# Layer-2 results of a mixture-of-experts kernel: through a DRAM scratch in 4 writes and 3 reads per expert, with the clearing of three PSUM banks at another place

## The chip, the cores and the metric

One core of a Trainium2 chip runs the whole program. The metric is the device time of one execution in microseconds (us); lower is better. Of each kernel some executions are timed, and one more is profiled.

## What is computed

The program is a linear attention followed by a mixture of 16 experts (4 groups of 4). Every token goes to exactly one expert, picked by two argmax steps. Cut to what matters here:

```
kv  = einsum('bhsd,bhse->bhde', k, v);  out = einsum('bhsd,bhde->bhse', q, kv)
x   = (out / rms(out) * g_norm), as 4608 tokens of 512 features
g   = argmax(x @ w_group);  e = argmax(x @ w_expert[g])          # one expert per token
out[token] = gate * (max(x[token] @ w1[g, e], 0) @ w2[g, e])     # 512 -> 1024 -> 512
```

All inputs and the output are float32. Each expert has 4 MB of weights.

## The kernel before

**Order of the work.** The attention and the routing come first, in an order that a planner writes out. Then the experts are taken by rank, that is by the number of their tokens: rank r is given room for CAPS[r] tokens, from 384 (rank 0) down to 256 (rank 15), and what is beyond goes to a loop at the end that does nothing on this input. Most of rank 0 is computed while the attention ends; what is left of it (128 tokens) and ranks 1 to 15 are the second part, which begins at line 1311. There the order of instructions on each engine is that in which the code is written.

**One rank** (loop at line 1376) has a layer 1 and a layer 2, each of 96 matmuls. A float32 product is made of three products of rounded values: ScalarE makes the rounded part (`whi`, `xh`, `hh`) and VectorE the rest (`wlo`, `xl`, `hl`). Layer 1 goes over 8 chunks f of the hidden features into PSUM tiles `ps`. Layer 2 (`layer2_by_feature`, line 1292) goes over 4 blocks d of the output features: 24 matmuls into one of three PSUM banks `psy`, in turn, then VectorE turns the block by 32 x 32 squares into the SBUF tile `yq` (line 1303). There is one `yq`, so the first such transpose of a rank waits until the results of the rank before have been moved out of it. In the order of VectorE the transposes stand between the splits of the next rank's weights and rows.

**The rows of x.** Three ranks are under way at any time. In layer 1 of rank r GpSimd gathers the rows of rank r+2 (`gather`), multiplies them by their factors (`scale`), and SyncE writes them to a DRAM scratch `xd` (`put_x`, 3 DMAs). At the start of layer 1 of rank r SyncE reads the rows of rank r+1 back as `xq` (`get_x`, 4 DMAs, in pieces of 512 bytes), so laid out that VectorE's transposes by squares (`turn_x`) make a whole transpose of it.

**The results.** `yq` holds the results of a rank by squares. `move_y` (line 1270) brings them to rows, `yo3`, by 16 DMAs from SBUF to SBUF in pieces of 512 bytes, and GpSimd scatters the rows of `yo3` to the output (`scatter_rows`), in layer 1 of the next rank, at f = 5 to 7. There are two `yo3`.

**The weights** come as four DMAs of 1 MB per rank (`wr`; `load_half`, line 207). Their 12 buffers are shared by the loaded and the split halves, so some loads wait until older ones are free: in layer 1 of rank r the two halves of w2 of rank r+1 are loaded (`load_next`), at the end of its layer 2 the two halves of w1 of rank r+2 (`load_a`).

**SyncE's queue** issues all of these DMAs but the gathers and scatters, in the written order. In a rank it is: 4 reads of `xq`, 16 moves of `yq`, 3 writes of `xd`, 2 loads of w2, then 2 loads of w1. Eight semaphores take turns for its DMAs, so a DMA waits at its issue until the one eight before it has landed.

**The banks.** The transposes take whole squares of 32 tokens, so they read up to 31 columns that no matmul wrote. Lines 1358 and 1359 clear columns 256 to 383 of the three banks once, after VectorE has prepared the rows of rank 1 (`turn_x`, `split_x`) and ahead of the last product of rank 0 (line 1364), 32 matmuls (line 299) that write the same banks.

Of the kernel before, what the change touches and what calls it, by code (L numbers as in the profile page):

```python
# [9 lines left out]
F32 = mybir.dt.float32  # L10
# [11 lines left out]
CAPS = [384, 364, 354, 330, 326, 312, 302, 300, 292, 290, 284, 274, 268, 264, 260, 256]  # L22
# [33 lines left out]
def tile_linattn_moe(ctx: ExitStack, tc: tile.TileContext, qm, qt, k, v, router, w1, w2, out):  # L56
    nc = tc.nc
    P = 128
    B, H, S, D = BATCH, HEADS, SEQ, HEAD_DIM
    NTOK, DM = out.shape  # L60
# [179 lines left out]
    def split_piece(w, p):  # L240
        for x, hi, lo in quarter(w, p):
            nc.scalar.copy(out=hi, in_=x)  # L242
            nc.vector.tensor_tensor(out=lo, in0=x, in1=hi.bitcast(F32), op=ALU.subtract)  # L243

    def blocks(cap):
        return [(j, min(P, cap - j * P)) for j in range((cap + P - 1) // P)]
# [5 lines left out]
    def scatter_rows(yo, rows, idx):  # L252
        sc = nc.gpsimd.indirect_dma_start(  # L253
            out=out, out_offset=bass.IndirectOffsetOnAxis(ap=idx[0:rows, :], axis=0), in_=yo[0:rows, :],
            in_offset=None, bounds_check=NTOK - 1, oob_is_err=False)
        tc.declare_no_dep(sc.ins, group=osc, reason="each token has a row of its own")
        tc.add_to_no_dep_group(osc, sc.ins)
# [3 lines left out]
    def by_quarter(x):  # L261
        return x.rearrange("p (a c i) -> p a c i", a=4, c=KC)

    def by_chunk(x):
        return x.rearrange("p (c a i) -> p a c i", a=4, i=32)

    def factors(x):

        return x[:, DM:RW].rearrange("p (c h) -> p h c", h=2).unsqueeze(2).unsqueeze(4).to_broadcast([P, 2, 2, KC, 32])

    def scale_rows(eng, xg, out_=None):

        x = by_quarter(xg[:, 0:DM])
        out_ = x if out_ is None else by_chunk(out_)
        for h in range(2):
            hs = slice(2 * h, 2 * h + 2)
            eng.tensor_tensor(out=out_[:, hs], in0=x[:, hs], in1=factors(xg)[:, h], op=ALU.mult)  # L277

    def split_h(hh, hl, ps):
        nc.scalar.activation(out=hh, in_=ps, func=AF.Relu)  # L280
        nc.vector.scalar_tensor_tensor(out=hl, in0=ps, scalar=0.0, in1=hh.bitcast(F32), op0=ALU.max, op1=ALU.subtract)  # L281

    def layer1(ps, w1, f, xh, xl):
        cs = slice((f % 4) * P, (f % 4 + 1) * P)
        _, wh, wl = w1[f // 4]
        three(ps, KC, lambda c: wh[:, c, cs], lambda c: wl[:, c, cs], lambda c: xh[:, c, :], lambda c: xl[:, c, :])
# [852 lines left out]
    with ExitStack() as ph:  # L1139
# [79 lines left out]
        psys = [ps_q.tile([P, 512], F32, name=f"psy{i}", tag=f"psy{i}") for i in range(3)]  # L1219
# [5 lines left out]

        def moves(cap):

            part = [slice(32 * i, 32 * i + 32) for i in range(4)]  # L1230
            return [(a, s_, part[a], part[s_], len(range(s_, (cap + 31) // 32, 4)))
                    for k in range(4) for s_ in range(4) for a in [(s_ + k) % 4]]

        def gather(r):
            xg = mp.tile([P, 3, RW], F32, name="xg")
            for j, _ in blocks(CAPS[r]):
                st["gather"] = gather_rows(xg[:, j], P, gidx[:, r, j:j + 1])
            xh = mp.tile([P, KC, 384], F32R, name="xh")
            xl = mp.tile([P, KC, 384], F32R, name="xl")
            return xg, xh, xl  # L1240

        def scale(r, g):
            for j, _ in blocks(CAPS[r]):
                scale_rows(nc.gpsimd, g[0][:, j])

        def put_x(r, g):
            for j, rows in blocks(CAPS[r] + -CAPS[r] % 32):
                nc.sync.dma_start(xd[r % 2][j * P:j * P + rows, :], g[0][0:rows, j, 0:DM])

        def get_x(r):  # L1250
            n = (CAPS[r] + 31) // 32
            xq = mp.tile([P, 12, P], F32, name="xq", bufs=1)
            for a in range(4):
                nc.sync.dma_start(xq[32 * a:32 * a + 32, 0:n, :],
                                  xd[r % 2][0:32 * n, a * P:(a + 1) * P].rearrange("(b i) f -> i b f", i=32))
            return xq, mp.tile([P, KC, 384], F32, name="xt", bufs=1)

        def turn_x(r, xq, xt, c):
# [4 lines left out]
        def split_x(r, g, xt, c):  # L1263

            x, xh, xl = (y[:, c, 0:CAPS[r]] for y in (xt, g[1], g[2]))
            nc.scalar.activation(out=xh, in_=x, func=AF.Copy, scale=g2[:, 0:1])  # L1266
            nc.vector.scalar_tensor_tensor(out=xl, in0=x, scalar=g2[:, 0:1], in1=xh.bitcast(F32), op0=ALU.mult,  # L1267
                                           op1=ALU.subtract)

        def move_y(r, yq):  # L1270
            yo = mp.tile([P, 3 * DM], F32, name="yo3", tag="yo3").rearrange("p (j f) -> p j f", j=3)
            pq = yq.rearrange("p (j s) f -> p j s f", s=4)
            for a, s_, pa, ps_, n in moves(CAPS[r]):
                nc.sync.dma_start(yo[ps_, 0:n, a * P:(a + 1) * P], pq[pa, 0:n, s_, :])  # L1274
            return [(yo[:, j], rows, gidx[:, r, j:j + 1]) for j, rows in blocks(CAPS[r])]

        def layer2_by_token(r, w2, hh, hl, side):
# [42 lines left out]
        scale_rows(nc.vector, xr, xs)  # L1320
        for j, _ in blocks(CAPS[1]):
            scale_rows(nc.vector, cur[0][:, j])
        put_x(1, cur)
        xq, xt = get_x(1)
        for i in range(2, 4):
            load_next(i)
# [28 lines left out]
        for c in range(KC):  # L1355
            turn_x(1, xq, xt, c)
            split_x(1, cur, xt, c)
        for x in psys:
            nc.vector.memset(x[:, DM // 2:384], 0.0)
        yo = mp.tile([P, DM], F32, name="yo", bufs=2)  # L1360
        for hf in range(2):
            ps = next_psy()
# [11 lines left out]
        todo, results = None, []  # L1374
        tables = overflow_tables()
        for r in range(1, NE):
            cap = CAPS[r]
            _, xh, xl = cur
            hh = mp.tile([P, FC, 384], F32R, name="hh", bufs=1)
            hl = mp.tile([P, FC, 384], F32R, name="hl", tag="hl", bufs=1)  # L1380
            if nxt:
                xq, xt = get_x(r + 1)
            if todo:
                results = move_y(*todo)
            for f in range(FC):
                if f in w1_at:
                    split_piece(w1c, w1_at[f])
                if f in w2_at:
                    split_piece(w2c, w2_at[f])
                ps = ps_h.tile([P, 512], F32, name="ps")  # L1390
                layer1(ps[:, 0:cap], w1c, f, xh[:, :, 0:cap], xl[:, :, 0:cap])
                split_h(hh[:, f, 0:cap], hl[:, f, 0:cap], ps[:, 0:cap])
                if r > 1:
                    next(tables, None)
                    next(tables, None)
                if f == 0:
                    nxt2 = gather(r + 2) if r + 2 < NE else None
                if nxt2 and f == 1:
                    scale(r + 2, nxt2)
                    put_x(r + 2, nxt2)  # L1400
                if nxt and f in (3, 5):
                    load_next((f + 1) // 2)
                if f >= 5 and results:
                    scatter_rows(*results.pop(0))
                if f == FC - 1 and r + 1 == NE:
                    nc.gpsimd.drain()
            nw1a, nw2a, load_a = weight_loads(eidx[0:1, r + 2:r + 3]) if nxt2 else (None, None, None)
            w1_at, w2_at = {}, {0: 0, 2: 1, 4: 2, 6: 3}

            def side(n, total, after):  # L1410
                if nxt is None:
                    return
                if not after:
                    split_piece(nw1, n)
                    if n < 2:
                        turn_x(r + 1, xq, xt, 2 * n)
                        turn_x(r + 1, xq, xt, 2 * n + 1)
                else:
                    for c in ([0], [1, 2], [3], [])[n]:
                        split_x(r + 1, nxt, xt, c)  # L1420
                    if n >= 2 and nxt2:
                        load_a(n - 2)

            if r + 1 == NE:
                layer2_by_token(r, w2c, hh, hl, side)
            else:
                todo = layer2_by_feature(r, w2c, hh, hl, side)
            cur, w1c, w2c = nxt, nw1, nw2
            nxt, nw1, nw2, load_next = nxt2, nw1a, nw2a, load_a
# [3 lines left out]
    with ExitStack() as ph:  # L1433
# [4 lines left out]
        with tc.For_i(0, nv, 1) as it:  # L1438
# [52 lines left out]
            yo = op.tile([P, DM], F32, name="yoo")  # L1491
# [57 lines left out]
```

## Time and profile before

| | us |
|---|---|
| median of 3 timed runs | 629.09 |
| lowest and highest of them | 622.66 and 629.69 |
| the profiled execution's own time | 625.29 |
| its span, first to last instruction | 623.6 |
| TensorE busy with matmuls | 562.0 (90%) |
| VectorE, ScalarE, GpSimd busy | 375.3, 267.2, 210.3 |
| mean granted TensorE clock | 0.954 |
| DMA, 156.70 MB | 251 GB/s |

The profile is of one execution. In its tables PE is TensorE, PEld its weight loads, DVE VectorE, ACT ScalarE, POOL GpSimd, SP SyncE; SPq is SyncE's sequencer with its DMA issues. A row of the waits gives an engine and a line, whom it waited for, the total in us, how often, and the longest. In a timeline a row has its start and its length in us, then engine, line, operation and tiles; square brackets hold the idle time before it and who ended it. A table of windows gives for each stretch the busy time of each engine with its instructions, then the granted clock (1.00 is full), the busy share of the 16 DMA engines, and what they moved.

### The profile page before, as it was taken

Reading aid. Unit: us, or ns where it says so; the run is one execution under the profiler, and the core shown is the slowest. Engines: PE = TensorE matmul, PEld = TensorE weight load, DVE = VectorE, ACT = ScalarE, POOL = GpSimd, SP = SyncE. Lnnn points to the kernel's source line nnn. Section 1 sums busy time; section 2 is a strip of 40 time slices with the busy share of each in tenths; the row PEclk is TensorE's granted clock in tenths of the full one; section 3 lists DMA queues with packets and bytes.
Section 4 is the critical chain, followed back from the end, with each engine's and each line's share of the span. In section 5 each row is a group of like instructions: output and inputs, shape, how many; then the busy total and the mean of one; then the engine's idle time right before and its main releaser. Section 6 shows DMA issues by size and latency. Waiting matters only on the chain.

```text
span 623.6 us, 13421 instructions
## 1 busy us (share of the span) xinstructions
PE 562.0 (90%) x5181; PEld 521.1 (84%) x5199; DVE 375.3 (60%) x786; ACT 267.2 (43%) x534; POOL 210.3 (34%) x281
## 2 busy tenths in 40 slices
PE   8888869999499999999999998979898979898895
PEld 4666757587189999999999997979898979798895
DVE  4235895862527686777677674657566565658470
ACT  0355645612225344544455453534353435345360
POOL 4032323245226235243144343334334243411103
PEclk9898999999889999999999999979998979798999
DMA  8999995648867769596959595969687777859541
GB/s 297 388 410 359 379 376 190 227 164 263 284 200 253 214 190 313 165 344 172 309 148 353 160 336 183 306 195 286 207 281 261 216 277 204 312 145 354 128 136 68
DMA packets 76788, 156.70 MB, mean 251 GB/s; under 512 B 10194, under 2 KB 49442, under 8 KB 65714
## 3 DMA queue, kind: packets, MB, share of 16 engines
q1 hardware_dynamic: 68752, 133.66, 66.3%
q0 software_dynamic: 7824, 22.11, 10.0%
q8 instruction: 42, 0.69, 0.4%
q10 hardware_dynamic: 146, 0.04, 0.1%
q14 instruction: 24, 0.20, 0.1%
HBM read 117.74 MB, written 29.31 MB: 236 GB/s over the span
## 4 chain that ended last, share of the span: by engine, by line
DMA 37%; PE 36%; SPq 14%; DVE 7%; issue 5%; ACT 1%; POOL 0%; POOLq 0%; DVEq 0%
DMA xq<-xd 20%; SPq L1274 12%; DMA wr<-in_w_dram 7%; PE warm L368 4%; DMA yo<-yq 3%; PE ps L311 3%; PE ps L307 3%; PE ps L306 3%; PE psy L311 3%; PE psy L307 3%; PE ops L521 3%; PE psy L306 3%; PE l L295 2%; DVE wlo L243 2%; PE kps L474 2%
## 5 line engine op out<-in xcount | busy, mean ns | idle before, releaser
L243 DVE TENSOR_TENSOR wlo<-wr,whi 128x1024 fp32r<-128x1024 f32 (+1 forms) x180 | 156.2, 895 | 36.6 <-ACT whi L242 34.4
L306 PE MATMUL psy<-hh,whi 128*128 128x364 f32 (+13 forms) x448 | 141.3, 315 | 22.4 <-DVE yq L1303 22.4
L307 PE MATMUL ps<-xl,whi 128*128 128x364 f32 (+14 forms) x480 | 144.2, 300 | 1.3 <-DVE xl L1267 1.3
L306 PE MATMUL ps<-xh,whi 128*128 128x364 f32 (+14 forms) x480 | 144.1, 300 | 0.4 <-DVE hl L281 0.3
L311 PE MATMUL ps<-xh,wlo 128*128 128x364 f32 (+14 forms) x480 | 144.2, 300 | 0.0
L307 PE MATMUL psy<-hl,whi 128*128 128x364 f32 (+13 forms) x448 | 140.3, 313 | 0.0
L311 PE MATMUL psy<-hh,wlo 128*128 128x364 f32 (+13 forms) x448 | 140.2, 313 | 0.0
L242 ACT CAST whi<-wr 128x1024 fp32r<-128x1024 f32 (+1 forms) x180 | 129.8, 757 | 19.5 <-DMA wr<-in_w_dram 19.5
L253 POOL DMA_INDIRECT out_dram<-yo,gall x45 | 47.9, 1064 | 204.4 <-DMA xd<-xg 99.8
L306 PEld LDWEIGHTS psy<-hh,whi 128*128 128x128 f32 x448 | 89.8, 201 | 24.2 <-DVE yq L1303 24.2
L280 ACT ACTIVATE hh<-ps 128x364 fp32r<-128x364 f32 (+14 forms) x120 | 49.8, 419 | 99.4 <-PE ps L311 97.2
L307 PEld LDWEIGHTS ps<-xl,whi 128*128 128x128 f32 x480 | 90.5, 189 | 1.8 <-DVE xl L1267 1.8
L306 PEld LDWEIGHTS ps<-xh,whi 128*128 128x128 f32 x480 | 90.9, 189 | 0.8 <-DVE hl L281 0.8
L277 POOL TENSOR_TENSOR xg<-xg 128x256 f32<-128x256 f32 x82 | 59.9, 755 | 93.2 <-DMA xg<-scr,gall 93.1
L311 PEld LDWEIGHTS ps<-xh,wlo 128*128 128x128 f32 x480 | 90.6, 189 | 0.0
L307 PEld LDWEIGHTS psy<-hl,whi 128*128 128x128 f32 x448 | 89.9, 201 | 0.0
L311 PEld LDWEIGHTS psy<-hh,wlo 128*128 128x128 f32 x448 | 89.8, 200 | 0.0
L1266 ACT ACTIVATE xh<-xt,rw 128x364 fp32r<-128x364 f32 (+14 forms) x60 | 32.6, 543 | 118.3 <-DVE xt L1260 105.3
L281 DVE SCALAR_TENSOR_TENSOR hl<-ps,hh 128x364 fp32r<-128x364 f32 (+14 forms) x120 | 54.8, 463 | 39.5 <-ACT hh L280 36.4
L1303 DVE STREAM_TRANSPOSE yq<-psy 128x320 f32<-128x320 f32 (+3 forms) x56 | 28.4, 508 | 80.1 <-DMA yo<-yq 62.9
L249 POOL DMA_INDIRECT xg<-scr,gall x44 | 57.3, 1302 | 13.3 <-issue 13.1
L368 PE MATMUL warm<-wide_b,ones_b 128*128 128x512 bf16 x124 | 37.0, 428 | 4.1 <-POOL wide_b L102 2.2
(255 smaller groups left out, 588.3 us busy)
## 6 DMA issues: line engine op xcount, KB each, us to landing
wr<-in_w_dram SPq DMA_DIRECT2D x64, 1024.0 KB
scr<-xo SPq DMA_DIRECT2D x36, 256.0 KB
m_q<-in_qm_dram SPq DMA_DIRECT2D x8, 1024.0 KB
xd<-xg SPq DMA_DIRECT2D x32, 256.0 KB
m_k<-in_k_dram SPq DMA_DIRECT2D x7, 1024.0 KB
m_v<-in_v_dram SPq DMA_DIRECT2D x7, 1024.0 KB
yo<-yq SPq DMA_DIRECT2D x116, 48.0 KB
yo<-yq SPq DMA_DIRECT2D x108, 32.0 KB
```

The source lines that it names most:

```text
L242: nc.scalar.copy(out=hi, in_=x)
L243: nc.vector.tensor_tensor(out=lo, in0=x, in1=hi.bitcast(F32), op=ALU.subtract)
L249: return nc.gpsimd.indirect_dma_start(out=xg[0:rows, 0:RW], out_offset=None, in_=src, in_offset=bass.IndirectOffsetOnAxis(ap=idx[0:rows, : ...
L253: sc = nc.gpsimd.indirect_dma_start(out=out, out_offset=bass.IndirectOffsetOnAxis(ap=idx[0:rows, :], axis=0), in_=yo[0:rows, :], in_offset ...
L277: eng.tensor_tensor(out=out_[:, hs], in0=x[:, hs], in1=factors(xg)[:, h], op=ALU.mult)
L280: nc.scalar.activation(out=hh, in_=ps, func=AF.Relu)
L281: nc.vector.scalar_tensor_tensor(out=hl, in0=ps, scalar=0.0, in1=hh.bitcast(F32), op0=ALU.max, op1=ALU.subtract)
L306: nc.tensor.matmul(ps, lhsT=stat_h(c), rhs=mov_h(c), start=(c == 0), stop=False)
L307: nc.tensor.matmul(ps, lhsT=stat_h(c), rhs=mov_l(c), start=False, stop=False)
L311: nc.tensor.matmul(ps, lhsT=stat_l(d), rhs=mov_h(d), start=False, stop=(d == n - 1))
L368: nc.tensor.matmul(st["warm"], lhsT=ones_b, rhs=wide_b, start=True, stop=True)
L1274: nc.sync.dma_start(yo[ps_, 0:n, a * P:(a + 1) * P], pq[pa, 0:n, s_, :])
```

## The change

Two things are edited. First, `move_y` and its table of 16 moves go. In their place `put_y` writes `yq` to one of two new DRAM scratches `yd` by 4 DMAs, at the place where `move_y` stood, and `get_y` reads it back into `yo3` as whole rows of 2 KB by 3 DMAs (128, 128 and the rest of the rows), at f = 2 of layer 1. `put_x` of rank r+2 moves from f = 1 to f = 4, behind the first load of w2. Second, the clearing of the banks moves from behind `split_x` of rank 1 to a place ahead of `put_x` of rank 1.

```diff
+    yd = [tc.dram_tile([3 * P, DM], F32, name=f"yd{i}") for i in range(2)]
...
-        def moves(cap):
-
-            part = [slice(32 * i, 32 * i + 32) for i in range(4)]
-            return [(a, s_, part[a], part[s_], len(range(s_, (cap + 31) // 32, 4)))
-                    for k in range(4) for s_ in range(4) for a in [(s_ + k) % 4]]
+        def quarter_rows(x, cap, a):
+            n = (cap + 31) // 32
+            return x[0:32 * n, a * P:(a + 1) * P].rearrange("(b i) f -> i b f", i=32)
...
-        def move_y(r, yq):
+        def put_y(r, yq):
+            for a in range(4):
+                nc.sync.dma_start(quarter_rows(yd[r % 2], CAPS[r], a), yq[32 * a:32 * a + 32, 0:(CAPS[r] + 31) // 32, :])
+
+        def get_y(r, yq):
             yo = mp.tile([P, 3 * DM], F32, name="yo3", tag="yo3").rearrange("p (j f) -> p j f", j=3)
-            pq = yq.rearrange("p (j s) f -> p j s f", s=4)
-            for a, s_, pa, ps_, n in moves(CAPS[r]):
-                nc.sync.dma_start(yo[ps_, 0:n, a * P:(a + 1) * P], pq[pa, 0:n, s_, :])
+            for j, rows in blocks(CAPS[r]):
+                nc.sync.dma_start(yo[0:rows, j], yd[r % 2][j * P:j * P + rows, :])
             return [(yo[:, j], rows, gidx[:, r, j:j + 1]) for j, rows in blocks(CAPS[r])]
...
             scale_rows(nc.vector, cur[0][:, j])
+        for x in psys:
+            nc.vector.memset(x[:, DM // 2:384], 0.0)
         put_x(1, cur)
...
             split_x(1, cur, xt, c)
-        for x in psys:
-            nc.vector.memset(x[:, DM // 2:384], 0.0)
         yo = mp.tile([P, DM], F32, name="yo", bufs=2)
...
             if todo:
-                results = move_y(*todo)
+                put_y(*todo)
...
                     scale(r + 2, nxt2)
-                    put_x(r + 2, nxt2)
+                if todo and f == 2:
+                    results = get_y(*todo)
                 if nxt and f in (3, 5):
                     load_next((f + 1) // 2)
+                if nxt2 and f == 4:
+                    put_x(r + 2, nxt2)
```

`get_x` uses `quarter_rows` too and does what it did.

The first place is SyncE's queue at the start of layer 1 of rank 2, with what each DMA waits for beside the order of the queue (DMAHW0 to DMAHW7 are the eight semaphores in turn; `xq<-xd` reads rows, `yo<-yq` moves results). Before:

```order
L1254 DMA xq<-xd_59 32x11x128 [waits DMAHW2_49,DMAHW1_49,DMAHW7_49,DMAHW0_49,DVE_49]
L1254 DMA xq<-xd_59 32x11x128 x3
L1274 DMA yo_2910<-yq 32x3x128 [waits DMAHW3_49,DVE_49]
L1274 DMA yo_2910<-yq 32x3x128 [waits DMAHW4_49]
L1274 DMA yo_2910<-yq 32x3x128 [waits DMAHW5_49]
L1274 DMA yo_2910<-yq 32x3x128 [waits DMAHW6_49]
L1274 DMA yo_2910<-yq 32x3x128 [waits DMAHW7_49]
L1274 DMA yo_2910<-yq 32x3x128 [waits DMAHW0_49]
L1274 DMA yo_2910<-yq 32x3x128 [waits DMAHW1_49]
L1274 DMA yo_2910<-yq 32x3x128 [waits DMAHW2_49]
```

Each move takes the next semaphore of the eight; the other eight moves follow in the same way, and each of those waits for one of the first eight. The same place in the changed kernel:

```order
L1253 DMA xq<-xd_59 32x11x128 [waits DMAHW3_49,DMAHW2_49,DMAHW7_49,DMAHW1_49,DVE_49]
L1253 DMA xq<-xd_59 32x11x128 [waits DMAHW0_49]
L1253 DMA xq<-xd_59 32x11x128 x2
L1270 DMA yd_61<-yq 32x12x128 [waits DVE_49]
L1270 DMA yd_61<-yq 32x12x128 [waits DMAHW4_49]
L1270 DMA yd_61<-yq 32x12x128 [waits DMAHW5_49]
L1270 DMA yd_61<-yq 32x12x128 [waits DMAHW6_49]
L1275 DMA yo_2994<-yd_61 128x512 [waits DMAHW6_49,DMAHW5_49,DMAHW7_49,DMAHW4_49,DMAHW3_49]
L1275 DMA yo_2994<-yd_61 128x512 [waits DMAHW0_49]
L1275 DMA yo_2994<-yd_61 108x512 [waits DMAHW1_49]
```

Four writes follow the reads of `xq`, and the first read of results waits for all four of them; whatever comes later in the queue waits behind it.

The second place is the same queue further on, from the results of rank 1 to the load of the index of the expert of rank 4 (`TENSOR_LOAD`; `xd<-xg` writes rows, `wr` is a half of w2). Before:

```order
L1274 DMA yo_2910<-yq 32x3x128 x16
L1248 DMA xd_58<-xg 128x512 x2
L1248 DMA xd_58<-xg 96x512
L209 ISA
L209 DMA wr_3026<-in_w_dram 128x2048
L209 ISA
L209 DMA wr_3072<-in_w_dram 128x2048
L204 TENSOR_LOAD eidx
```

And in the changed kernel:

```order
L1270 DMA yd_61<-yq 32x12x128 x4
L1275 DMA yo_2994<-yd_61 128x512 x2
L1275 DMA yo_2994<-yd_61 108x512
L210 ISA
L210 DMA wr_3016<-in_w_dram 128x2048
L1247 DMA xd_58<-xg 128x512 x2
L1247 DMA xd_58<-xg 96x512
L210 ISA
L210 DMA wr_3065<-in_w_dram 128x2048
L205 TENSOR_LOAD eidx
```

23 DMAs stand here and at the reads of `xq` before (4, 16, 3) and 14 now (4, 4, 3, 3), and the first half of w2 stands ahead of the writes of rows.

The third place is VectorE's queue between the scaling of the rows of rank 1 and its layer 1 (`hT` is what the last product of rank 0 reads, `psy` are the banks). Before:

```order
L1346 COPY hT<-ps 128x4x128 x2
L1260 STREAM_TRANSPOSE xt<-xq 128x384
L1267 SCALAR_TENSOR_TENSOR xl<-xt,rw,xh 128x364
L1260 STREAM_TRANSPOSE xt<-xq 128x384
L1267 SCALAR_TENSOR_TENSOR xl<-xt,rw,xh 128x364
L1260 STREAM_TRANSPOSE xt<-xq 128x384
L1267 SCALAR_TENSOR_TENSOR xl<-xt,rw,xh 128x364
L1260 STREAM_TRANSPOSE xt<-xq 128x384
L1267 SCALAR_TENSOR_TENSOR xl<-xt,rw,xh 128x364
L1359 MEMSET psy_2443 128x128
L1359 MEMSET psy_2444 128x128
L1359 MEMSET psy_2442 128x128
```

In the changed kernel:

```order
L278 TENSOR_TENSOR xg<-xg 128x256 x6
L1325 MEMSET psy_2444 128x128
L1325 MEMSET psy_2445 128x128
L1325 MEMSET psy_2446 128x128
L244 TENSOR_TENSOR wlo<-wr_2463,whi 128x4x256 x2
L1349 COPY hT<-ps 128x4x128 x2
L1258 STREAM_TRANSPOSE xt<-xq 128x384
```

The three clearings have moved ahead of the two splits, the two copies of `hT` and all eight steps on the rows. On TensorE, ScalarE and GpSimd the order is as before.

More of the change, by code (lines that the diff above doesn't have):

```diff
@@ L1253, in get_x @@
             for a in range(4):
-                nc.sync.dma_start(xq[32 * a:32 * a + 32, 0:n, :],
-                                  xd[r % 2][0:32 * n, a * P:(a + 1) * P].rearrange("(b i) f -> i b f", i=32))
+                nc.sync.dma_start(xq[32 * a:32 * a + 32, 0:n, :], quarter_rows(xd[r % 2], CAPS[r], a))
             return xq, mp.tile([P, KC, 384], F32, name="xt", bufs=1)
```

## The prediction

> **What bounds the kernel now.** I read the page first, then a table of windows cut at the first matmul of each rank's layer 1, then the waits, then one rank in the timeline and the chain.
>
> The page says that TensorE is nearly full, and that its clock is not always full in the second half:
>
> ```profile
> PE 562.0 (90%) x5181; PEld 521.1 (84%) x5199; DVE 375.3 (60%) x786; ACT 267.2 (43%) x534; POOL 210.3 (34%) x281
> ...
> PEclk9898999999889999999999999979998979798999
> ```
>
> The table shows where. One row per rank, here ranks 3 to 15:
>
> ```profile
> core 0: us, PE busy (x) PEld busy (x) DVE busy (x) ACT busy (x) POOL busy (x), PEclk, DMA share, GB/s
> 246.66:275.27 28.61, 28.61 (x195) 28.61 (x193) 21.01 (x48) 13.52 (x24) 9.53 (x10) 1.00 0.78 246
> 275.27:304.06 28.79, 28.79 (x194) 28.79 (x193) 19.71 (x40) 13.55 (x24) 8.21 (x8) 1.00 0.83 232
> 304.06:331.46 27.40, 27.40 (x195) 27.40 (x194) 19.80 (x32) 13.43 (x24) 10.70 (x12) 1.00 0.76 218
> 331.46:357.91 26.45, 26.45 (x195) 26.45 (x194) 16.40 (x29) 11.81 (x22) 8.12 (x11) 1.00 0.77 241
> 357.91:386.88 28.97, 26.51 (x194) 26.26 (x193) 17.50 (x32) 12.30 (x24) 10.93 (x12) 1.00 0.79 251
> 386.88:420.13 33.25, 28.78 (x195) 28.30 (x194) 20.42 (x37) 14.63 (x28) 13.17 (x15) 0.90 0.80 254
> 420.13:448.34 28.21, 26.37 (x195) 26.13 (x194) 16.56 (x29) 11.64 (x23) 11.06 (x11) 1.00 0.76 237
> 448.34:478.53 30.19, 27.26 (x195) 26.79 (x194) 19.52 (x35) 14.26 (x27) 12.34 (x14) 0.94 0.80 262
> 478.53:509.34 30.81, 26.62 (x195) 26.41 (x193) 18.42 (x34) 12.96 (x24) 12.08 (x13) 0.89 0.76 241
> 509.34:538.90 29.56, 26.59 (x194) 26.37 (x193) 18.36 (x34) 12.90 (x24) 13.05 (x13) 0.89 0.77 248
> 538.90:568.00 29.10, 25.75 (x194) 25.12 (x193) 16.79 (x31) 12.38 (x24) 6.96 (x8) 0.93 0.75 245
> 568.00:594.65 26.65, 24.83 (x194) 24.62 (x193) 17.12 (x34) 12.87 (x25) 2.97 (x3) 0.94 0.73 232
> 594.65:623.60 28.95, 21.93 (x194) 21.73 (x192) 10.21 (x21) 8.65 (x21) 4.89 (x5) 0.96 0.27 85
> ```
>
> Up to rank 6 TensorE is busy in every microsecond, and a rank takes time in proportion to its tokens: 111.25 us for the 330 + 326 + 312 + 302 = 1270 tokens of ranks 3 to 6, or 0.0876 us a token. From rank 7 on the tokens go on falling, from 300 to 260, but a rank keeps taking some 27 to 33 us: something of constant length sets the pace. The waits name it:
>
> ```profile
> DVE yq L1303 <- DMA yo<-yq: 62.9, 10, 7.6
> ...
> PE psy L306 <- DVE yq L1303: 22.4, 8, 4.2
> ...
> PE psy L299 <- DVE psy L1359: 10.3, 1, 10.3
> ```
>
> TensorE waits for VectorE's transposes into `yq`, and they wait for the moves out of `yq`. Rank 9 in the timeline of SyncE's queue:
>
> ```profile
> 412.17 1.49 SPq L1248 DMA_DIRECT2D xd<-xg  x3
> 413.93 2.71 SPq L209 DMA_DIRECT2D wr<-in_w_dram  x4
> 416.82 5.33 SPq L1254 DMA_DIRECT2D xq<-xd  x4
> 422.32 20.38 SPq L1274 DMA_DIRECT2D yo<-yq  x16
> 442.81 1.48 SPq L1248 DMA_DIRECT2D xd<-xg  x3
> ```
>
> From the chain of work that ended last, the last move of the rank before and the reads of `xq` (from issue to landing):
>
> ```profile
> 411.46 1.86 DMA yo<-yq
> ...
> 416.82 18.23 DMA xq<-xd
> ```
>
> The first transpose of rank 9 in VectorE's timeline, one of rank 8's matmuls in TensorE's, and two windows of TensorE's clock behind that wait:
>
> ```profile
> 444.40 0.52 DVE L1303 STREAM_TRANSPOSE yq<-psy 128x320 f32<-128x320 f32 x1 [7.31 <-DMA yo<-yq]
> ```
>
> ```profile
> 414.21 0.61 PE L306 MATMUL psy<-hh,whi 128*128 128x292 f32 x1 [3.81 <-DVE yq L1303]
> ```
>
> ```profile
> 414.20:420.13 5.93, 5.92 (x25) 5.92 (x26) 5.93 (x11) 3.05 (x5) 4.58 (x5) 0.51 0.89 301
> 420.13:433.20 13.07, 13.07 (x99) 13.07 (x98) 9.82 (x17) 6.92 (x15) 5.91 (x6) 1.00 1.06 349
> ```
>
> The 16 moves take 20.38 us to issue. A move waits for the DMA eight before it, so the middle ones wait for the reads of `xq`, which stand behind four weight loads and land 18.23 us after their issue; then the last dozen go out one by one. Only then come the writes of rows and all four weight loads, in a burst, and `xq` queues behind them again. That is a loop of SyncE's queue, some 30 us long whatever TensorE has to do. It costs twice: the wait itself (3.81 us here), and then a granted clock of 0.51 for 5.93 us.
>
> **The banks.** The last row of the waits is a single stall. VectorE reaches the clearing only after the rows of rank 1:
>
> ```profile
> 162.61 0.69 DVE L1346 COPY hT<-ps 128x512 f32<-128x512 f32 x1 [0.21 <-PE ps L1345]
> 165.56 0.58 DVE L1260 STREAM_TRANSPOSE xt<-xq 128x384 f32<-128x384 f32 x1 [2.26 <-DMA xq<-xd]
> ...
> 172.06 0.60 DVE L1267 SCALAR_TENSOR_TENSOR xl<-xt,rw,xh 128x364 fp32r<-128x364 f32 x1 [0.67 <-ACT xh L1266]
> 172.68 0.45 DVE L1359 MEMSET psy<- 128x128 f32 x3
> ```
>
> The window of the product that waits for it, and ScalarE's last use of one of these banks in the part before:
>
> ```profile
> 172.90:182.05 9.15, 9.15 (x32) 7.71 (x33) 0.23 (x2) 0.37 (x1) 0.00 (x0) 0.74 0.89 242
> ```
>
> ```profile
> 149.78 0.37 ACT L1115 COPY yos<-l 128x256 f32<-128x256 f32 x1 [3.65 <-PE l L299]
> ```
>
> The product's operand `hT` is there at 163.3, but TensorE stands idle for 10.3 us until the banks are cleared at 172.9, and then needs 9.15 us at a mean clock of 0.74 before layer 1 of rank 1 starts at 182.05.
>
> **The change part by part.** *Clearing.* The three memsets (0.45 us) now follow the scaling; they can run once ScalarE has emptied an older tile at 150.15, and VectorE is idle there. The first product into a bank, at 150.2, may start up to 0.5 us later. The product of 32 matmuls then starts at about 163.7 and takes 6.8 us (9.15 x 0.74, the full clock) to 9.15; I take 7.5, since the gap that lowered the clock is gone. It ends at 171.2. Layer 1 needs the last `xl` (172.66) only at its tenth matmul, some 1.5 us in, so it starts at about 171.7: **10.3 us earlier**, between 9.4 (if it needed that `xl` first) and 10.9. The wait after that is for `xq`, which does not move.
>
> *The stall on `yq`.* Without it, ranks 7 to 14 take 0.0876 x (300 + 292 + 290 + 284 + 274 + 268 + 264 + 260 = 2232 tokens) = 195.5 us. They take 594.65 - 357.91 = 236.7 now. If TensorE never waits: **41.2 us less**, waits and low clock together.
>
> *Does it never wait?* Follow a rank of 274 tokens (24 us) from the start of its layer 1. `put_y` can issue when the last transpose is done, at 1 us; the reads of `xq` and the two loads of w1 ahead of it were issued in the layer 2 before and are through by about 2; its bytes take what those of the moves take, whose price is in a stretch where nothing else ran, 436 to 443 us:
>
> ```profile
> q1 hardware_dynamic: 1075, 0.46, 29.6%
> ```
>
> 29.6% of 7 us for 0.46 MB, so 2.7 us for 0.6 MB. With 1 us until the landing is known, `yq` is free at 6 to 7 us, and it is wanted when layer 1 (12) and the first block of layer 2 (3) are done: a reserve of about 9 us. In this wait SyncE stands at the first `get_y`; queued behind it are the other reads, the first half of w2, the writes of rows, the second half of w2 and the w1 loads. The first half of w2 is issued at 8 instead of behind 16 moves (it is wanted at 24), the rows of rank r+2 right after (wanted one rank on), so all of these come earlier than now. GpSimd's scatter, which now waits until layer 2, comes at 10. The shorter queue also spreads the weights: half of them go in layer 1 rather than all four at once.
>
> *What the transfers need instead.* From the table, length times DMA share summed over ranks 7 to 13 is 163 us, so 23.3 us of transfers per rank. The 16 moves turn into writes of the same bytes in the same 512-byte pieces (no change, if a piece costs the same), and `get_y` adds 0.56 MB, 1.6 us at the 349 GB/s of the row above. Between the last byte of `put_y` and the first of `get_y` SyncE's DMAs pause: a single small move takes 1.86 us from issue to landing, of which its bytes are 0.2, so 1.7. Together 26.6 us per rank. TensorE needs 26.3, 25.6, 25.4, 24.9, 24.0, 23.5 and 23.1 us for ranks 7 to 13, so the transfers fall behind by 0.3 + 1.0 + 1.2 + 1.7 + 2.6 + 3.1 + 3.5 = 13.4 us. Of this the reserve takes 9: **4.4 us come back as stalls** in the last ranks.
>
> No row shows a write of 512 bytes to DRAM. From below: if the pause is filled by GpSimd's transfers, 24.9 us per rank, 4.1 us behind in all, no stall. From above I take the write of rows, three DMAs of 0.79 MB in all:
>
> ```profile
> 151.44 7.06 DMA xd<-xg
> ```
>
> At that pace 0.6 MB take 5.4 us instead of 2.7, and a rank 29.3. I take the moves' price: same pieces, same queue, and that row includes the traffic ahead of it. The Trainium skill speaks for something between: in "DMA: Bandwidth & Descriptors", section "Why small descriptors are slow (HBM only)", transfers within SBUF are free of a penalty that pieces in HBM pay, some 3 cycles on each packet. For the 16 beats of 512 bytes that would be an estimated 19%, so 0.5 us per rank and some 3.5 us more in all; no run here shows it yet.
>
> *Sum*, against the profiled execution's span: 623.6 - 10.3 - 41.2 + 4.4 = 576.5. The tail from rank 15 on (28.95 us) I leave as it is. Its own time is 1.7 above its span, so 578.2; it lies 3.8 below the median of the runs and 2.6 above the lowest. I forecast **580**, half of that 3.8 added; its own range is 570 to 590.
>
> **The rivals.** *A: the transfers become the bound.* If a rank's transfers take 28 us, they fall behind from rank 5 on, by 0.7 + 1.5 + 1.7 + 2.4 + 2.6 + 3.1 + 4.0 + 4.5 + 4.9 = 25.4 us; less 9 that is 16.4 us of stalls, and two stretches of low clock of 2.9 each bring 22: 594 for the span, 598 timed (at 29.3, 604). For it: DMA shares of 0.76 to 0.80 already at 30 us per rank. Against: 0.83 in rank 4 without a stall.
>
> *B: the move does not free `yq` earlier.* `put_y` still stands behind `xq` in the same queue, and if its landing waits out the weights as `xq` does now (18 us), the loop stays. Only the clearing pays: 613 span, 615 to 617 timed. Against: the loads ahead of `xq` are then two, not four.
>
> *C, slower: DRAM writes of 512 bytes are dear.* SyncE's whole queue stands behind the landing of `put_y`. At three times the moves' price (8 us) a rank takes 32; ranks 1 to 14 then take 32.6 + 13 x 31.9 = 447 us instead of 412.6, so 623.6 - 10.3 + 35 = 648, timed 650. It decides from 2.4 times on, where the ranks eat up the 10.3 us. Against: the reads of `xq` and the moves use the same pieces, and the stretch at 349 GB/s is full of them.
>
> **How the numbers follow.** The forecast has 0.73, A 0.17, B 0.06, C 0.03; 0.01 is left for what I don't see. Range: from 570 (no stall, and runs at the low end of their spread) to 606 (A at its dearest). A measurement of this kernel tells about 2%, 12.6 us: faster by more is the forecast, A and a remainder, 0.91; within it B, 0.06; slower C, 0.03.
>
> **What would show it.** Layer 1 of rank 1 starts near 171.7, and the wait of line 299 for the clearing is gone. Ranks 7 to 14 take 0.0876 us a token at a clock of 1.00, with waits on `yq` near zero; DMA share goes to 0.9 and more in ranks 10 to 13. `put_y` lands 6 to 7 us into a rank. It is wrong if ranks 3 to 6 get longer than 28.6, 28.8, 27.4 and 26.5 us, if TensorE waits on `yq` or on weights for more than 10 us in all, or if a rank's length stops falling with its tokens.

## The result, and the profile after

The changed kernel takes 599.03 us (median of 4 runs, 592.25 to 600.12) beside 627.07 for the kernel before on the same chip: a ratio of 0.954, with an interval of 0.944 to 0.963. It is faster by 28 us, where the forecast of 580 wanted 47 to 49. 599 lies outside the forecast's own range (570 to 590) and inside the whole one (570 to 606), at the time that rival A names (598).

The profiled execution took 600.12 us with a span of 598.4. From its page, TensorE's busy time and its clock in 40 slices:

```profile
PE 554.5 (93%) x5199; PEld 513.6 (86%) x5199; DVE 382.0 (64%) x786; ACT 266.0 (44%) x534; POOL 211.5 (35%) x281
...
PEclk9998998999999999999999999999989897989999
DMA packets 78897, 165.32 MB, mean 276 GB/s; under 512 B 8084, under 2 KB 47332, under 8 KB 67824
```

TensorE is fuller (93% for 90%). In the second part of the program the clock has four holes, from slice 30 on, where before it had five from slice 27 on. The DMA engines move 8.6 MB more. The table of windows, one row per rank, ranks 7 to 15:

```profile
core 0: us, PE busy (x) PEld busy (x) DVE busy (x) ACT busy (x) POOL busy (x), PEclk, DMA share, GB/s
...
347.30:373.50 26.20, 26.20 (x194) 26.20 (x193) 18.88 (x32) 13.32 (x24) 9.87 (x11) 1.00 0.88 254
373.50:399.80 26.30, 26.30 (x195) 26.30 (x194) 19.40 (x32) 12.11 (x22) 9.38 (x11) 1.00 0.89 254
399.80:429.00 29.20, 26.34 (x193) 26.11 (x193) 18.35 (x32) 12.92 (x24) 9.77 (x11) 1.00 0.88 281
429.00:458.80 29.80, 27.34 (x194) 27.10 (x193) 18.94 (x32) 12.94 (x24) 12.20 (x12) 0.94 0.88 266
458.80:488.10 29.30, 26.14 (x195) 25.92 (x194) 18.17 (x32) 12.75 (x24) 9.71 (x11) 0.94 0.86 251
488.10:518.80 30.70, 27.00 (x195) 26.56 (x194) 18.83 (x32) 13.15 (x26) 15.27 (x15) 0.89 0.92 308
518.80:545.50 26.70, 24.91 (x195) 24.70 (x194) 17.58 (x32) 12.19 (x24) 6.57 (x7) 0.94 0.83 255
545.50:569.70 24.20, 23.30 (x195) 23.09 (x194) 17.46 (x32) 12.72 (x24) 3.79 (x3) 1.00 0.87 275
569.70:598.40 28.70, 22.69 (x194) 22.38 (x192) 8.51 (x17) 8.49 (x20) 5.00 (x6) 0.98 0.35 117
```

Ranks 7 and 8, which took 28.97 and 33.25 us before, now run at TensorE's pace. Ranks 9 to 12 take 29 to 31 us again, whatever their tokens; rank 13 takes 26.7 and rank 14 24.2. Against the kernel before, layer 1 of rank 1 starts at 171.9 instead of 182.05 (10.2 less), ranks 1 to 6 take 175.4 for 175.9, ranks 7 to 14 222.4 for 236.7 (14.3 less), and the tail 28.7 for 28.95.

The waits, of all engines and then of SyncE's queue, show what took the place of the wait on `yq`:

```profile
...
ACT whi L243 <- DMA wr<-in_w_dram: 55.3, 15, 5.5
DVE hl L282 <- ACT hh L281: 49.6, 59, 1.5
DVE wlo L244 <- ACT whi L243: 49.6, 36, 5.3
...
DVE yq L1304 <- PE psy L312: 27.0, 32, 1.5
...
PE ps L307 <- DVE hl L282: 14.9, 7, 3.5
```

```profile
SPq L1253 <- DMA xd<-xg: 54.7, 16, 7.1
SPq L1275 <- DMA yd<-yq: 46.1, 38, 4.0
...
SPq L1270 <- DMA wr<-in_w_dram: 21.9, 15, 4.4
```

VectorE's transposes now wait for TensorE's products; of their 62.9 us of waits for the moves out of `yq`, 1.0 us is left (for `put_y`). What has grown is ScalarE's wait for weights. Before it was:

```profile
ACT whi L242 <- DMA wr<-in_w_dram: 19.5, 16, 3.3
```

It waits for the halves of w2, which it rounds by quarters in layer 1, between its steps on `hh`. While it waits, `hh` waits, then VectorE's `hl`, then TensorE: 14.9 us direct. Behind four of the stalls, in ranks 10 to 13, the granted clock is 0.50 for 3.4 us, in rank 12 for 6.8. ScalarE in rank 9, with what ended its idle time in brackets:

```profile
401.46 1.14 ACT L243 CAST whi<-wr 128x512 fp32r<-128x512 f32 x2 [5.51 <-DMA wr<-in_w_dram]
...
408.58 1.14 ACT L243 CAST whi<-wr 128x512 fp32r<-128x512 f32 x2 [4.93 <-DMA wr<-in_w_dram]
```

SyncE's queue from the `get_y` in rank 9 to the one in rank 10 (rank 10 starts at 429.0):

```profile
419.48 1.29 SPq L1275 DMA_DIRECT2D yo<-yd  x3
421.02 0.36 SPq L210 DMA_DIRECT2D wr<-in_w_dram  x1
421.49 3.10 SPq L1247 DMA_DIRECT2D xd<-xg  x3
424.79 3.33 SPq L210 DMA_DIRECT2D wr<-in_w_dram  x3
433.37 2.99 SPq L1253 DMA_DIRECT2D xq<-xd  x4
436.41 9.43 SPq L1270 DMA_DIRECT2D yd<-yq  x4
449.62 1.18 SPq L1275 DMA_DIRECT2D yo<-yd  x3
```

And from the chain of work that ended last, start and length:

```profile
427.70 17.81 DMA wr<-in_w_dram
...
445.53 4.00 DMA yd<-yq
449.62 0.34 SPq L1275
```

This is a loop again, 30.1 us from one `get_y` to the next. Behind `get_y` all four weight loads go out within 9 us. The last of them lands 17.81 us after its issue. The last of the four writes of `put_y` needs that load's semaphore (eight take turns), so it is issued only at 445.53 and has landed 4.00 us later. In those 4 us SyncE stands at `get_y` with everything else behind it. The DMA engines, cut at that place:

```profile
419.40:423.00 3.60, 3.60 (x28) 3.60 (x28) 3.27 (x7) 2.35 (x5) 0.58 (x1) 1.00 0.64 185
423.00:426.00 3.00, 3.00 (x24) 3.00 (x23) 2.21 (x5) 2.18 (x3) 2.25 (x2) 1.00 0.65 188
426.00:447.00 21.00, 18.54 (x128) 18.30 (x127) 11.60 (x20) 7.67 (x17) 9.46 (x11) 0.92 1.00 315
447.00:448.00 1.00, 1.00 (x9) 1.00 (x8) 0.52 (x2) 0.55 (x1) 0.00 (x0) 1.00 0.64 177
448.00:451.00 3.00, 3.00 (x25) 3.00 (x24) 2.71 (x6) 1.77 (x3) 0.00 (x0) 1.00 0.14 29
```

They are full for 21 us, stand almost still for 3 us (a share of 0.14), and are two thirds full for 6.6 us behind the `get_y` of 419.48. Behind the next one the share is 0.98 and 0.91 (451 to 455), so that this third part is not the same in every rank. SyncE's longest wait in total is another: the reads of `xq` wait for the landing of the writes of rows, 54.7 us where it was 13.7 before. Here it falls into the stretch in which the engines are full (it ends at 433.37), and in experiment 7, where `put_x` alone moves, it is 45.7 us without a change in time. In rank 2 `get_y` is issued 8 us into the rank, in rank 8 at 16.8, in rank 10 at 20.6 (449.62 - 429.0): the loop is longer than TensorE's 26 us, and falls back until TensorE stalls.

### The profile page after: what moved, and what is told of

Its sections match the earlier page's. It is cut to its first block, busy times and chain, and to the rows that moved or that the text cites. A ratio compares the mean times of both kernels' runs of the same rounds, so it can differ in the third digit from the quotient of the medians.

```text
span 598.4 us, 13267 instructions
## 1 busy us (share of the span) xinstructions
PE 554.5 (93%) x5199; PEld 513.6 (86%) x5199; DVE 382.0 (64%) x786; ACT 266.0 (44%) x534; POOL 211.5 (35%) x281
## 4 chain that ended last, share of the span: by engine, by line
PE 59%; DMA 26%; issue 6%; SPq 3%; DVE 3%; ACT 1%; POOL 1%; POOLq 0%; DVEq 0%; ACTq 0%
DMA wr<-in_w_dram 17%; PE ps L307 7%; PE psy L307 7%; PE psy L312 7%; PE psy L308 7%; PE ps L312 7%; PE ps L308 7%; PE ops L522 3%; PE kps L475 3%; DMA yd<-yq 3%; PE warm L369 3%; PE l L296 2%; DMA m_v<-in_v_dram 2%; PE psy L300 2%; DMA xs<-scr,sidx 1%
## 5 line engine op out<-in xcount | busy, mean ns | idle before, releaser
L307 PE MATMUL ps<-xh,whi 128*128 128x364 f32 (+14 forms) x480 | 148.2, 309 | 14.9 <-DVE hl L282 14.9
L312 PE MATMUL psy<-hh,wlo 128*128 128x364 f32 (+13 forms) x448 | 135.1, 302 | 0.0
L307 PE MATMUL psy<-hh,whi 128*128 128x364 f32 (+13 forms) x448 | 135.0, 301 | 0.0
L308 PE MATMUL psy<-hl,whi 128*128 128x364 f32 (+13 forms) x448 | 134.9, 301 | 0.0
L254 POOL DMA_INDIRECT out_dram<-yo,gall x45 | 53.7, 1193 | 182.2 <-DMA yo<-yd 151.3
L308 PEld LDWEIGHTS ps<-xl,whi 128*128 128x128 f32 x480 | 93.7, 195 | 0.0
L307 PEld LDWEIGHTS psy<-hh,whi 128*128 128x128 f32 x448 | 84.5, 189 | 0.0
L308 PEld LDWEIGHTS psy<-hl,whi 128*128 128x128 f32 x448 | 84.4, 188 | 0.0
L312 PEld LDWEIGHTS psy<-hh,wlo 128*128 128x128 f32 x448 | 84.4, 188 | 0.0
L250 POOL DMA_INDIRECT xg<-scr,gall x44 | 50.2, 1141 | 13.3 <-issue 13.1
L1264 ACT ACTIVATE xh<-xt,rw 128x364 fp32r<-128x364 f32 (+14 forms) x60 | 32.6, 543 | 48.8 <-DVE xt L1258 48.8
L1304 DVE STREAM_TRANSPOSE yq<-psy 128x320 f32<-128x320 f32 (+3 forms) x56 | 28.7, 512 | 28.3 <-PE psy L312 27.0
```

Source lines behind the costliest of these rows:

```text
L250: return nc.gpsimd.indirect_dma_start(out=xg[0:rows, 0:RW], out_offset=None, in_=src, in_offset=bass.IndirectOffsetOnAxis(ap=idx[0:rows, : ...
L254: sc = nc.gpsimd.indirect_dma_start(out=out, out_offset=bass.IndirectOffsetOnAxis(ap=idx[0:rows, :], axis=0), in_=yo[0:rows, :], in_offset ...
L307: nc.tensor.matmul(ps, lhsT=stat_h(c), rhs=mov_h(c), start=(c == 0), stop=False)
L308: nc.tensor.matmul(ps, lhsT=stat_h(c), rhs=mov_l(c), start=False, stop=False)
L312: nc.tensor.matmul(ps, lhsT=stat_l(d), rhs=mov_h(d), start=False, stop=(d == n - 1))
```

## The experiments

Each kernel is timed in rounds with the kernel before on its chip, which took 626.5, 627.6 and 628.4 us in the three sets.

**1. The clearing alone, in the kernel before.**

```diff
+        for x in psys:
+            nc.vector.memset(x[:, DM // 2:384], 0.0)
         put_x(1, cur)
...
-        for x in psys:
-            nc.vector.memset(x[:, DM // 2:384], 0.0)
```

> The kernel before with nothing changed but the place of the clearing. Theory (the two edits are independent, the clearing is worth the 10.2 us that layer 1 of rank 1 starts earlier in the changed kernel): span 613 to 614, layer 1 of rank 1 at 172, ratio 0.984; ranks 7 to 14 still take about 237 us. Rival (what is won at the start is lost again, because ranks 7 to 14 are paced by transfers and not by TensorE): span above 619, ratio 0.992 or more, with ranks 7 to 14 above 242 us.

617.61 us, ratio 0.985 (0.981 to 0.989): 7 to 12 us less. The span of 616.5 lies between the theory's (613 to 614) and the rival's (above 619). Ranks 7 to 14 took 235.9 us in its trace, as before (236.7), and the wait on `yq` stayed. From its waits:

```profile
DVE yq L1303 <- DMA yo<-yq: 63.7, 10, 7.4
...
PE psy L306 <- DVE yq L1303: 20.8, 9, 4.1
```

**2. The trip through DRAM alone:** the changed kernel with the clearing at its old place (the same lines moved back).

> The changed kernel with the clearing back at its old place, so the round trip through DRAM alone. Theory (independent edits): layer 1 of rank 1 at 182, the rest as in the changed kernel, span 608 to 609, ratio 0.97; ranks 7 to 14 take about 222 us. Rival (the late start gives the transfers of the first ranks more time, so fewer stalls come later): span 600 to 604 and ranks 7 to 14 below 216 us.

609.06 us, ratio 0.974 (0.969 to 0.979). Ranks 7 to 14 took 219.1 us, nearer to the theory's 222 than to the rival's 216 and less, and the late weights are there without the clearing. From its waits:

```profile
ACT whi L243 <- DMA wr<-in_w_dram: 56.2, 18, 5.1
...
PE psy L300 <- DVE psy L1360: 9.0, 1, 9.0
```

0.985 x 0.974 = 0.960 beside 0.954 (0.944 to 0.963) for both: within the interval the two edits add up, and the loss of some 20 us against the forecast sits in the trip.

**3. The changed kernel with the first load of w2 ahead of `get_y`.** SyncE waits for `put_y` as before, but with 1 MB of weights already issued.

```diff
+                if nxt and f == 1:
+                    load_next(2)
                 if todo and f == 2:
                     results = get_y(*todo)
-                if nxt and f in (3, 5):
-                    load_next((f + 1) // 2)
+                if nxt and f == 5:
+                    load_next(3)
```

> The changed kernel with the load of the first half of w2 issued between the writes and the reads of results, so that the DMA engines have 1 MB of work while SyncE waits for the writes to land. Theory (in ranks 9 to 13 a rank takes 25 to 26 us of transfers plus a pause of some 4 us around the round trip, in which the whole queue stands): the pause goes, 3 to 4 us per rank off ranks 9 to 13 until TensorE is the bound again, span 581 to 588, ratio 0.93 to 0.94, waits for weights below 15 us. Rival (the bytes and their 512-byte pieces alone set the pace, the pause only moves): span 594 to 600, waits for weights as before near 55 us.

577.48 us, ratio 0.923 (0.919 to 0.927), better than the theory's 0.93 to 0.94. One load moved gives back 22 us by the medians and 19 by the ratios. Ranks 8 and 11 of its trace; TensorE is busy throughout and at full clock, and the last two columns say that DMA is full too:

```profile
374.70:401.00 26.30, 26.30 (x195) 26.30 (x194) 18.94 (x32) 13.14 (x24) 12.43 (x12) 1.00 1.00 327
...
452.70:477.00 24.30, 24.30 (x194) 24.30 (x193) 18.16 (x32) 12.95 (x24) 11.62 (x12) 1.00 0.97 305
```

**4. `get_y` issued by GpSimd**, so that SyncE's queue has no wait for `put_y` at all.

```diff
-                nc.sync.dma_start(yo[0:rows, j], yd[r % 2][j * P:j * P + rows, :])
+                nc.gpsimd.dma_start(yo[0:rows, j], yd[r % 2][j * P:j * P + rows, :])
```

> The changed kernel with the reads of results issued by GpSimd, so that SyncE never waits for the landing of the writes and goes on with weights and rows. Theory (the pause): as with the load moved forward, span 581 to 589, ratio 0.93 to 0.945. Rival (bytes and pieces alone): span 594 to 600. A third way: GpSimd, which then waits for the landing, gathers later, rows come late, and the span is above 600.

576.50 us, ratio 0.921 (0.917 to 0.924), again better than the theory. GpSimd now takes the wait, and has room for it. Experiments 3 and 4 beat both kernels, with ranks 7 to 14 at 198.5 and 198.6 us; they move the same bytes as the changed kernel. The bytes alone are thus not what cost the 22 us; where the queue stands, and what stands behind it, matters.

**5. Experiment 4 with the bytes of `put_y` written twice.**

```diff
+    yx = [tc.dram_tile([P, 12, 2 * P], F32, name=f"yx{i}") for i in range(2)]
...
+            nc.sync.dma_start(yx[r % 2][:, 0:(CAPS[r] + 31) // 32, 0:P], yq[:, 0:(CAPS[r] + 31) // 32, :])
```

> The kernel with the reads of results on GpSimd, and the bytes of put_y written a second time, in the same pieces of 512 bytes, by one more DMA into a DRAM scratch that nobody reads. That kernel took 576.5 us, with DMA shares that come to 24.3 us per rank in ranks 7 to 13. If a piece of 512 bytes costs in DRAM what a move inside SBUF costs (2.7 us for the bytes of a rank), a rank needs 27.0 us of transfers against 23.1 to 26.3 of TensorE: some 13.5 us behind in all, less the reserve of about 10, so 578 to 592 us. If such writes are dear (5.4 us and more for a rank), a rank needs 29.7 and falls behind by about 38 us: 603 us and more.

578.33 us, ratio 0.922 (0.917 to 0.927), at the low end of what cheap pieces allow. Rank 9 of experiment 4, then the same rank here; the last two columns are the DMA share and GB/s:

```profile
399.60:425.70 26.10, 26.10 (x194) 26.10 (x193) 18.75 (x32) 13.02 (x24) 14.39 (x18) 1.00 0.96 319
```

```profile
400.80:426.90 26.10, 26.10 (x194) 26.10 (x193) 18.84 (x32) 13.13 (x24) 13.74 (x16) 1.00 1.02 340
```

Length times share over ranks 7 to 13 goes from 24.3 to 26.0 us per rank: 0.6 MB more in pieces of 512 bytes cost 1.6 us, less than the 2.7 of the prediction. In this traffic rival C's dear writes do not show. (The share can pass 1 because transfers overlap in it.)

**6. Experiment 4 with `put_x` back at f = 1**, so that SyncE waits there, ahead of w2, for GpSimd's scaling.

```diff
                     scale(r + 2, nxt2)
+                    put_x(r + 2, nxt2)
...
-                if nxt2 and f == 4:
-                    put_x(r + 2, nxt2)
```

> The kernel with the reads of results on GpSimd, and put_x back at f = 1, ahead of the first load of w2: in SyncE's order the writes of rows stand directly behind put_y. They wait for GpSimd's scaling, which ends some 13.9 us into a rank, so the load of w2 is issued at about 14 instead of 6 us. Theory (any wait in which SyncE's queue stands ahead of the loads costs, whatever it is for): the first halves of w2 come late again, 588 to 605 us. Rival (only the wait for put_y mattered, the place of put_x does nothing): 573 to 582 us.

577.91 us, ratio 0.921 (0.916 to 0.927): the theory missed. The load of w2 does go out late, 13.6 us into rank 10, and nothing stalls. From SyncE's timeline (rank 10 starts at 426.3):

```profile
427.09 8.77 SPq L1270 DMA_DIRECT2D yd<-yq  x4
436.79 2.88 SPq L1247 DMA_DIRECT2D xd<-xg  x3
439.94 6.11 SPq L210 DMA_DIRECT2D wr<-in_w_dram  x4
```

This wait in the queue cost little, because the transfers already issued kept the engines busy. SyncE goes on at 436.79, 1.3 us before the first of the writes of `put_y` lands (438.11). From 436 to 443 us the DMA share is 0.70, not near zero, and before and after it is 1.07 and 1.01.

**7. The kernel before with `put_x` at f = 4**, the moves kept: the order of the queue without the trip.

```diff
-                    put_x(r + 2, nxt2)
...
+                if nxt2 and f == 4:
+                    put_x(r + 2, nxt2)
```

> The kernel before with nothing changed but the place of put_x: at f = 4, behind the first load of w2, as in the change; the 16 moves stay. Theory (the moves hold SyncE's queue for some 20 us of each rank, and behind them GpSimd's scaling has long been done, so the writes of rows wait for nothing): no change, 618 to 632 us. Rival (a part of the change's gain is the new order of the queue and not the trip through DRAM): 605 to 615 us.

630.69 us, ratio 1.002 (0.998 to 1.005): no change. The new place of `put_x`, which is part of the first edit, brings nothing by itself in the kernel before; the gain of the trip is the trip's.

**8. Experiment 4 with a short stand:** one read of 512 bytes on SyncE, nobody's operand.

```diff
+            z = mp.tile([1, P], F32, name="stand", bufs=2)
+            nc.sync.dma_start(z, yd[r % 2][0:1, 0:P])
```

> The kernel with the reads of results on GpSimd (576.5 us), and one read of 512 bytes of the DRAM scratch of results on SyncE at f = 2, which nobody uses: the wait for the landing of put_y is back in SyncE's queue, the bytes of get_y are not. Theory (the changed kernel loses its 22 us because SyncE's queue stands there while the DMA engines run dry): 590 to 602 us, and first halves of w2 come late again. Rival (it was the bytes of get_y in SyncE's queue, or their place among the loads): 574 to 582 us.

579.64 us, ratio 0.921 (0.914 to 0.927): the theory missed again. But this was not the stand of the changed kernel. The read touches only the columns of the first of the four writes, so SyncE goes on when that one has landed, 1 to 2 us before the fourth (ranks 8 to 12). The next experiment makes it whole.

**9. Experiment 4 with the full stand:** as 8, but the 512 bytes come from the columns of all four writes.

```diff
+            nc.sync.dma_start(z.rearrange("o (a f) -> o a f", a=4),
+                              yd[r % 2][0:1, :].rearrange("o (a f) -> o a f", a=4)[:, :, 0:32])
```

> The kernel with the reads of results on GpSimd (576.5 us), and on SyncE at f = 2 one read of 512 bytes that nobody uses, 128 bytes from the columns of each of the four writes of put_y, so that SyncE's queue stands until all four have landed, as in the change; the small read that waited for the first of the four alone left the time at 579.6 us. Theory 1 (the length of the stand decides: with the full one the DMA engines run dry for some 3 us of each rank and the queue's loop is longer than TensorE's rank): 590 to 602 us, with late halves of w2. Theory 2 (what decides is that get_y's 0.56 MB go through SyncE's queue ahead of the weights; on GpSimd's queue they fill the pause): 574 to 584 us.

583.64 us, ratio 0.929 (0.922 to 0.937). From its waits, and its windows around the landing of `put_y` in ranks 10 and 11:

```profile
ACT whi L243 <- DMA wr<-in_w_dram: 23.6, 11, 3.5
```

```profile
417.00:440.00 23.00, 23.00 (x173) 23.00 (x172) 15.95 (x28) 12.09 (x23) 11.24 (x13) 1.00 1.03 345
440.00:444.00 4.00, 4.00 (x32) 4.00 (x31) 3.56 (x6) 2.00 (x4) 1.58 (x4) 1.00 0.12 30
444.00:467.00 23.00, 23.00 (x181) 23.00 (x180) 16.19 (x28) 11.19 (x21) 10.95 (x11) 1.00 1.04 339
467.00:470.00 3.00, 3.00 (x26) 3.00 (x26) 1.46 (x4) 1.66 (x3) 1.51 (x4) 1.00 0.16 48
```

Here the pause stands alone, 3 to 4 us at 0.12 to 0.16, and it is real: the loop is 26.9 us long (issues at 388.13 and 495.86, four ranks), w2 comes late, and TensorE stalls in ranks 12 and 14. Ranks 7 to 14 take 205.7 us, 7.1 more than in experiment 4 (the intervals of the two ratios, 0.922 to 0.937 and 0.917 to 0.924, still touch). That is 30% of the 23.9 us that the changed kernel loses in these ranks. The time lies just inside theory 2's 574 to 584, but the late weights are theory 1's: each has a part.

**10. The changed kernel with only the first read of `get_y` ahead of w2,** the other two behind it.

```diff
-            for j, rows in blocks(CAPS[r]):
-                nc.sync.dma_start(yo[0:rows, j], yd[r % 2][j * P:j * P + rows, :])
+            def read(k):
+                for j, rows in blocks(CAPS[r])[k]:
+                    nc.sync.dma_start(yo[0:rows, j], yd[r % 2][j * P:j * P + rows, :])
+            read(slice(0, 1))
...
                     load_next((f + 1) // 2)
+                if todo and f == 3:
+                    read(slice(1, 3))
```

> The changed kernel (599.0 us) with only the first of the three reads of get_y (0.26 MB) ahead of the first load of w2; the other two follow behind that load, all on SyncE. The stand is as long as in the change. Theory 1 (the length of the stand decides): 592 to 602 us. Theory 2 (the bytes of get_y ahead of w2 decide): half of them have gone, 577 to 590 us. Neither if it is the number of DMAs behind the stand, which is unchanged.

583.37 us, ratio 0.924 (0.912 to 0.936), with single runs from 577.2 to 586.1: inside theory 2's 577 to 590. Its windows, cut in the same way:

```profile
417.00:439.00 22.00, 22.00 (x166) 22.00 (x165) 15.77 (x27) 11.23 (x23) 10.53 (x12) 1.00 1.03 352
439.00:443.00 4.00, 4.00 (x32) 4.00 (x31) 3.10 (x7) 2.32 (x4) 0.29 (x1) 1.00 0.27 72
```

The pause is the same, and behind it the engines are full at once. The stand with the first read behind it costs about what the stand alone costs (583.6); it is the other two reads ahead of w2, 0.3 MB, that take the time from 583 to 599. What the loops look like, from `get_y` (or the small read) of rank 8 to that of rank 12, with length times DMA share from windows cut there. Each loop moves 8.0 MB:

| kernel | loop, us | length times share | idle |
|---|---|---|---|
| changed: full stand, three reads ahead of w2 | 29.4 | 25.9 | 3.5 |
| 10: full stand, one read ahead | 27.1 | 24.3 | 2.7 |
| 9: full stand, reads on GpSimd | 26.9 | 24.2 | 2.7 |
| 3: w2 ahead of the stand, then three reads | 25.9 | 25.4 | 0.5 |
| TensorE, ranks 8 to 11 | 25.6 | | |

In experiments 9 and 10 the idle time is the stand; in the changed kernel a part of it lies behind the stand (the share of 0.64 above). The third column is not a fixed price of the bytes: the same 8.0 MB come to 24.2 in one kernel and to 25.9 in another. It is high in the two kernels in which the three reads stand together on SyncE, and experiment 3 has 25.4 and no stall, because hardly any of its loop is idle. So the changed kernel loses by two terms together, the idle 3.5 us and some 1.7 us more of transfer time. With the idle time gone (experiment 3) all of the loss is gone; with the longer transfers gone (9 and 10) some two thirds of it. Why the same bytes take longer there no run settles.

## Why the prediction was right, and where it was not

**The clearing: right.** 10.3 us were forecast, 10.2 came: layer 1 starts at 171.9 (171.7 forecast), and the product's wait for the clearing goes from 10.3 us to 0.8. That the number is so close is partly luck: the product starts 1.4 us later than forecast (165.06 for 163.7), because rank 0's work ahead of it ends later; it takes 7.17 us (7.5 taken), and layer 1 follows it without the 0.5 us that were allowed for `xl`. Experiments 1 and 2 confirm the gain apart.

**The stall on `yq`: right.** Of the transposes' wait for a DMA 1.0 us is left, ranks 7 and 8 run at TensorE's pace, and without any stall (experiments 3 and 4) ranks 7 to 14 take 198.5 us. The forecast was 195.5; the 3.0 us are the step "0.0876 us a token", which ranks 8 to 12 do not follow (see the end). `put_y` landed 6 to 8 us into ranks 2 to 4, near the forecast, but 20 us into rank 10: there rival B's mechanism is at work, the landing waits for the weights ahead. It costs little on `yq`: in rank 10 the first transpose comes at 449.66, just behind the landing at 449.5. The 1 us that was allowed until a landing is known came from no row; from the last bytes to the landing the trace has 0.3 to 0.4 us in ranks 2 to 4.

**The transfers: the step that failed.** "Together 26.6 us per rank", from which 13.4 us behind and, after the reserve of 9, "4.4 us come back as stalls". The loop was 29.4 us, and 23.9 us came back (222.4 against 198.5). Three parts:
- The pause, the larger error. 1.7 us were taken from a single small move. A loop of the changed kernel has 3.5 us of idle transfers, 1.8 more: four writes must land, not one, and the last of them is issued only when the last w1 load has landed, since it needs that load's semaphore. Whether it would land sooner with a semaphore of its own no run tested. Experiment 9 prices the whole stand at 7.1 us.
- The transfers themselves. 24.9 us were forecast, 25.9 measured, 1.0 more. The prediction put `get_y`'s 0.56 MB at a flat 1.6 us wherever they stood; with the reads apart or on GpSimd the loop has 24.3 or 24.2.
- The reserve. Some 10 us for the 9 forecast (stalls follow a `get_y` that is issued 17 to 18 us into a rank, as in rank 8 here and rank 11 of experiment 9, and it starts at 8), but it was counted for the wrong tile. What is late first is w2, which stands behind `get_y` in SyncE's queue. The prediction had that time ("issued at 8", "wanted at 24"), and did not ask what becomes of that 8 when `put_y` itself slips.

The sum over the ranks turned a small error into a large one: 29.4 - 26.6 = 2.8 us per loop, over the seven ranks 7 to 13, is 20 us. That this fits the missing 19.5 (23.9 - 4.4) so well is partly luck, since 29.4 is the mean of loops from 27.3 to 30.9.

Rival A named the time, 598, but not quite for its reason. It wanted 28 us of transfers per rank; there are 25.9, and the DMA engines are idle for 3.5 us of each loop. Its other figure does not follow from its own count: at 29.3 us the ranks fall 38.2 us behind, and less 9, with 5.8 of low clock, that comes to 611, not 604. The upper end of the range rests on it.

**Rival C and the price of 512 bytes: refuted.** (Its "2.4 times" is 2.3 by its own formula: 32.6 + 13 x 30.0 = 422.9.) The writes of `put_y` cost no more than the moves did. In a stretch of the changed kernel where hardly anything else is under way (446 to 449.6), 0.43 MB of them take 46.4% of 3.6 us, so 2.3 us for 0.6 MB, beside the 2.7 of the moves; in experiment 5 a rank's bytes added 1.6 us. The Trainium skill's penalty for small pieces in HBM ("DMA: Bandwidth & Descriptors", section "Why small descriptors are slow (HBM only)") would have been some 0.5 us per rank by the prediction's estimate; no run here shows a premium.

**The signs.** The clock of 1.00 that was forecast for ranks 7 to 14 came in ranks 7, 8, 9 and 14; in 10 to 13 it is 0.89 to 0.94. DMA shares of 0.9 and more in ranks 10 to 13 were forecast; they are 0.88, 0.86, 0.92 and 0.83. In experiments 3 and 4 they are 0.94 to 1.02. There the forecast's time comes out too (577 us beside 580), partly by luck: the ranks take 3.0 us more than forecast, and the 4.4 us of stalls do not come. "TensorE waits ... on weights for more than 10 us in all" was a sign of being wrong, and by the chain through ScalarE and VectorE it was met (14.9 us).

## What to carry to other kernels

A DMA that waits for another one's landing stops the whole queue that issues it, here for 3 to 4 us under load and not for the 1.7 of a lone transfer. Try the next large load ahead of it, or an issue from an engine with room: with the same bytes, either was worth some 20 us here. Where a forecast compares two loops that differ by 1 or 2 us, compute the loop of the queue with its waits, over all ranks, before trusting the gain of the wait removed.

## What the hardware showed that I had not expected

- A rank's length on TensorE does not follow its tokens one by one. Without stalls (experiment 4) ranks 7, 8 and 9 (300, 292 and 290 tokens) take 26.3, 26.2 and 26.1 us, and rank 11 (274) takes 24.3. A price per token from longer ranks is 3 us short over eight ranks. Why the length falls in steps no run shows.
- With several kinds of transfers issued at once, the core moved 339 to 352 GB/s for 22 or 23 us on end (experiments 9 and 10), against a mean of 276 in the changed kernel, whose engines at a share of 1.00 moved 315 (426 to 447 us).
